# Queries and keys of the last two batches as pairs of float16 parts, turned by DMA, in an attention and expert kernel on one core

## The chip, the cores and the metric

The program runs on one core of a Trainium2 chip. Its engines work side by side, each on its own list of instructions in a fixed order: TensorE (PE; its weight loads are listed as PEld), VectorE (DVE), ScalarE (ACT), GpSimd (POOL), and SyncE (SP), which here does nothing but issue DMAs. They wait for each other by semaphores. The metric is device microseconds of one execution; before the change it is 641.41 us (median of 3 runs, 641.22 to 641.45).

## The reference

Causal attention over 4 batches, 12 heads, 448 positions and 64 elements a head, and behind it a product of two gates and two more matrix products, all in float32:

```
scores = where(mask, -1e9, (q @ k.T) / sqrt(64))
attn   = exp(scores - max) / (sum + 1e-9)
x      = (attn @ v), heads side by side        # 1792 x 768
h      = ((x @ w1) * (x @ w2)) @ w3            # w1, w2: 768 x 1024, w3: 1024 x 1024
out    = h @ w_out                             # 1024 x 768
```

Queries and keys are normal numbers, scaled by 0.7453 and 0.7659, so scores are a few units large and the softmax is not flat.

## The kernel before

First w3 and w_out are multiplied into one matrix (`w34`, L689, float32). Then each batch b goes through two dense stages: `gate(b)` multiplies x by w1 and w2 (L813 to L815: three float16 products for each float32 one, since x and w are kept as a high and a low float16 part), and `project(b)` multiplies by the joined matrix (L873 to L875, three float16 products again). Ahead of each gate, `norms(b)` takes a bound of x (L764, 24 matmuls); it needs x of the whole batch, so its place in the trace shows where the attention of batch b is over.

The attention is cut into 24 pairs of heads, 6 to a batch (`pair`). A pair loads q and k (L403, the helper of every DMA that SP issues), turns them on TensorE (L457: 8 float32 transposes against the identity) and copies them out of PSUM (L461 on ACT or L462 on DVE) into `qkt`, with one head on partitions 0 to 63 and the other on 64 to 127. Scores come in 7 blocks: for each head three of 384, 256 and 128 columns (L495), and one for the last 64 rows of both (L493). Each block is one of the four PSUM banks `sc`. VectorE masks the block, scales it and takes its maximum (L499), which frees the bank; ScalarE takes the exponential (L503); the rows are divided by their sum and split in two float16 parts (`soft`, L528 to L535). The parts are turned by DMA (`pt`, `ptt`) and meet the values in L556 and L561.

Where an instruction stands is set by a planner. `Program.add` takes a due time, the engines that could do the work with a cost each, and what is read and written; `Program.order` then plays the program through and hands each engine a list. The due times come from the numbers in `PLAN`. The result is that pairs of batch b + 1 lie scattered among the gate and projection matmuls of batches b - 1 and b. SP's list is as fixed as the others: a DMA whose data isn't ready holds up all DMAs behind it.

Helpers that matter below: `squares` (ACT: sum of squares, L355), `root_scale` (a one-column float32 matmul against ones, L367, and three small DVE instructions, L370 to L375, that give a power of two near the norm and its inverse), `scaled` (L381 ACT, L382 DVE or L384 POOL: the high float16 part) and `remainder` (DVE, L390: the low part). They serve values and weights before the change.

Of the kernel before, what the change touches and what calls it, by code (L numbers as in the profile page):

```python
# [12 lines left out]
F32 = mybir.dt.float32  # L13
# [13 lines left out]
PLAN = dict(nc=11, wstep=2.3205, soft=49.445, w0=118.4, w34=0.5037, ab=1.5277, out=0.179, gap=16.057, lat=37.703, begin=100.181, wlead=94.567, urgent=13.056, flex=96.023, sc=-27.259, vo=62.311, av=-129.283, x=-15.194, qlead=-18.284, rlead=-5.245, v0=30.056, v1=123.832, gram=2, nf=3, h0=3, hv=5, ns=7, wo0=-132.371, wo1=27.123, wom=21.268, w3a=15.279, w3l=17.856, wd=16.165, wh=-60.261, wl=58.537, fin=8.526, ev=-0.539, po=[-24.2, -29.15, -19.26, 10.49, -17.08, -21.38, -42.72, -39.55, -25.07, -1.21, -22.27, 20.91, 0.72, -56.42, -27.16, -10.64, -22.5, -16.12, -21.26, -21.97, -35.13, 2.64, -7.32, 4.13], wo=[-28.62, 5.45, -16.93, 42.18, 23.33, -12.43, 22.11, -20.21], w3=[-35.5, -43.06, -39.69, 7.92, 8.15, -9.78, -9.89, -29.26], tw=[-16.09, -51.07, -16.26, 0.98, -3.04, -29.34, -21.69, -23.59, -23.52, -22.71, -68.85, 16.04, -16.6, -4.06, -30.21, 7.83], slack=0.7, pflex=42.748)
# [169 lines left out]
def t_mm(n, least=0):  # L197
    return max(n / 2.4 + 2, least) / 1000
# [3 lines left out]
def tile_causal_attention_moe(ctx: ExitStack, tc: tile.TileContext, q, k, v, w1, w2, w3, wo, out):  # L202
    nc = tc.nc
# [32 lines left out]
    def ring(shape, dt, name, n):  # L236
        return Ring(name, fixed(shape, dt, name, n))
# [198 lines left out]
    OFF = (0, P, 3 * P)  # L436
    UP = 2.0**14

    def pair(p):
# [6 lines left out]
        for i, src in ((1, k), (0, q)):  # L446
            dma(qk[0:QP, i], src[b, hs].rearrange("h (p r) d -> p r h d", r=4),
                T - PLAN["qlead"], (), [qkk + (i,)], 2 * S * D * 4, rate=181e3)


        qt, qtk = qkt.next()
        for i in (1, 0):
            ps, key = prog.lease("sc", "tr")

            def turn(i=i, ps=ps):
                for r in range(4):
                    nc.tensor.transpose(ps[:, r:S:4], qk[0:QP, i, r].rearrange("p h d -> p (h d)"), ident[0:QP, 0:QP])  # L457

            prog.add(T + 0.1 * (1 - i), (PE, 4 * t_mm(2 * QP), turn), [qkk + (i,)], [key, qtk + (i,)])
            prog.add(T + 0.5, [  # L460
                (ACT, t_act(S, True), lambda i=i, ps=ps: nc.scalar.copy(out=qt[:, i], in_=ps[:, :S])),  # L461
                (DVE, t_dve(S), lambda i=i, ps=ps: nc.vector.tensor_copy(qt[:, i], ps[:, :S])),  # L462
            ], [key], [qtk + (i,)])

        vs, vsk, _, _ = vsc[b]
        v2, v2k = v16.next()
# [15 lines left out]
        def scores(u, due):  # L482
            i, c, w, lo = place(u)
            ps, key = prog.lease("sc")
            (t32, tk) = heads[i]
            o = t32[:, lo : lo + w]
            m = mask_t if i == 2 else mask[:, (2 - c) * P :]

            def products():
                for j in range(2):  # L490
                    rows = slice(j * D, (j + 1) * D)
                    if i == 2:
                        nc.tensor.matmul(ps[rows, :w], qt[rows, 0, 3 * P : S], qt[rows, 1, 0:w], start=True, stop=True)  # L493
                    elif i == j:
                        nc.tensor.matmul(ps[:, :w], qt[rows, 0, c * P : (c + 1) * P], qt[rows, 1, 0:w], start=True, stop=True)  # L495

            prog.add(due, (PE, 0.9 if i == 2 else max(2 * t_mm(w) + 0.1, 0.31), products),
                     [qtk + (1,), qtk + (0,)], [key, tk + (c,)] + ([tk] if p < 2 else []))
            prog.add(due + 0.4, (DVE, t_dve(w) + 0.09, lambda: nc.vector.tensor_tensor_reduce(  # L499
                out=o, in0=ps[:, :w], in1=m, scale=minus, scalar=-NEG,  # L500
                op0=ALU.add, op1=ALU.min, accum_out=mx[:, u : u + 1])),
                [key, "minus", "mask_t" if i == 2 else "mask"], [mk + (u,), tk + (c,)] + ([tk] if p < 2 else []))
# [394 lines left out]
    with w0 as w0p:  # L897
        w34(w0p)
        for half in range(2):
            at = len(prog.ops)  # L900
            take_v(0, half, starts[0] + PLAN["v0"] + 1.5 * half)
            hold(at, PLAN["hv"] + half)
        for p in range(NP):
            at = len(prog.ops)
            pair(p)
            hold(at, PLAN["h0"] + p)
            if p % 3 == 2:
                take_v(1, p // 3, starts[p] + PLAN["v1"])
# [63 lines left out]
```

## Time and profile before

| what | value |
|---|---|
| median of 3 runs | 641.41 us |
| profiled execution | 642.41 us, span of the trace 640.6 us |
| PE busy | 601.3 us, 94% of the span |
| DVE, ACT, POOL busy | 405.5, 318.7, 175.0 us |
| mean granted TensorE clock | 0.974 of 2.4 GHz |

The trace is of one execution. Spans of matmuls overlap, since they are pipelined, so sums over their mean durations exceed the time they take; the chain of waits, which gives each moment to one instruction, has the time that each one adds.

### The profile page before, as it was taken

The page shows a single profiled execution, that of the slowest core. Times are in us where ns is not written, and L with a number is a line of the kernel's source. Part 1 is how long each engine was busy: PE and PEld are TensorE (multiplying, and loading weights), DVE is VectorE, ACT ScalarE, POOL GpSimd, SP SyncE. Part 2 cuts the span into 40 slices and gives each one's busy share as a digit, 9 for nine tenths or more (in the row PEclk, how much of TensorE's full clock was granted, in tenths as well). Part 3 has the DMA queues.
Part 4 walks back from the last instruction along what each step waited for, and adds up shares of the span by engine and source line. Part 5 has one row for each costly group of instructions (what it writes and reads, how often), then busy time and mean ns, then how long its engine had stood idle before and what let it go on. Part 6 is the DMA issues. An engine that isn't in the chain of part 4 may idle for free.

```text
span 640.6 us, 10699 instructions
## 1 busy us (share of the span) xinstructions
PE 601.3 (94%) x3892; PEld 342.3 (53%) x3892; DVE 405.5 (63%) x1048; ACT 318.7 (50%) x739; POOL 175.0 (27%) x129
## 2 busy tenths in 40 slices
PE   3799969987989999999999999999999999999997
PEld 1454545655545555565655556555555556555564
DVE  7966999999989889866543358846528861212200
ACT  7546988587666867446331336635425441111111
POOL 5643754641554524313100023311102210000000
PEclk9899978988889999999999999999999999999999
DMA  8899596464888949759610139797107616000011
GB/s 340 248 235 226 130 235 169 133 186 111 162 153 170 189 103 154 129 102 185 141 30 19 40 76 176 152 172 143 29 2 150 125 23 124 26 1 1 0 50 49
DMA packets 198836, 78.29 MB, mean 122 GB/s; under 512 B 179840, under 2 KB 195712, under 8 KB 198784
## 3 DMA queue, kind: packets, MB, share of 16 engines
q1 hardware_dynamic: 198784, 77.61, 54.3%
q8 instruction: 30, 0.49, 0.3%
q14 instruction: 22, 0.18, 0.1%
HBM read 43.78 MB, written 5.51 MB: 77 GB/s over the span
## 4 chain that ended last, share of the span: by engine, by line
PE 74%; DVE 14%; issue 5%; ACT 4%; DMA 2%; POOL 0%; SPq 0%; DVEq 0%; ACTq 0%; POOLq 0%
PE sc L495 8%; PE mm L813 7%; PE mm L814 7%; PE mm L815 7%; PE mm L873 4%; PE mm L875 4%; PE mm L874 4%; PE mm L689 3%; PE tr L813 3%; PE tr L814 3%; PE tr L815 3%; PE av L561 3%; PE sc L493 3%; PE sc L689 2%; PE sc L457 2%
## 5 line engine op out<-in xcount | busy, mean ns | idle before, releaser
L532 POOL TENSOR_SCALAR ph<-p,rc 128x256 f16<-128x256 f32 (+2 forms) x47 | 52.8, 1128 | 162.2 <-DVE rc L513 66.4
L814 PE MATMUL mm<-xt,w 128*128 128x448 f16 x258 | 91.4, 354 | 1.9 <-DVE xt L573 1.9
L813 PE MATMUL mm<-xt,w 128*128 128x448 f16 x258 | 91.6, 355 | 0.4 <-ACT xt L570 0.2
L815 PE MATMUL mm<-xt,w 128*128 128x448 f16 x258 | 91.6, 355 | 0.0
L503 ACT ACTIVATE p<-p,mx 128x384 f32<-128x384 f32 (+2 forms) x144 | 71.7, 499 | 37.9 <-DVE mx L499 37.7
L499 DVE CUSTOM_DVE_ANT_0 p<-sc,mask,minus 128x384 f32<-128x384 f32 (+2 forms) x144 | 64.0, 480 | 30.6 <-PE sc L495 29.9
L495 PE MATMUL sc<-qkt 64*128 64x384 f32 (+2 forms) x288 | 72.8, 415 | 5.2 <-DVE mx L499 2.7
L689 PE MATMUL mm<-wof,w3t 128*128 128x384 f32 x192 | 73.3, 522 | 3.5 <-POOL wof L598 3.5
L535 DVE SCALAR_TENSOR_TENSOR ph<-p,rc,ph 128x384 f16<-128x384 f32 (+2 forms) x144 | 67.1, 509 | 3.6 <-ACT ph L530 2.3
L495 PEld LDWEIGHTS sc<-qkt 64*128 64x128 f32 x288 | 41.5, 190 | 40.3 <-issue 9.7
L813 PEld LDWEIGHTS <-w 128*128 128x128 f16 x384 | 38.2, 100 | 38.4 <-issue 5.5
L815 PEld LDWEIGHTS <-w 128*128 128x128 f16 x384 | 37.7, 98 | 38.0 <-issue 3.5
L814 PEld LDWEIGHTS <-w 128*128 128x128 f16 x384 | 37.8, 98 | 30.8 <-issue 1.1
L689 PEld LDWEIGHTS mm<-wof,w3t 128*128 128x128 f32 x192 | 36.6, 203 | 25.8 <-issue 4.7
L873 PE MATMUL mm<-w34h,arena 128*128 128x384 f16 x152 | 49.8, 327 | 0.0
L875 PE MATMUL mm<-w34h,arena 128*128 128x384 f16 x152 | 49.5, 326 | 0.0
L874 PE MATMUL mm<-w34l,arena 128*128 128x384 f16 x152 | 49.5, 326 | 0.0
L813 PE MATMUL tr<-xt,w 128*128 128x448 f16 x126 | 44.9, 357 | 0.0
L814 PE MATMUL tr<-xt,w 128*128 128x448 f16 x126 | 44.9, 356 | 0.0
L815 PE MATMUL tr<-xt,w 128*128 128x448 f16 x126 | 44.9, 356 | 0.0
L839 ACT CAST arena<-g 128x448 f16<-128x448 f32 x21 | 11.8, 564 | 57.4 <-DVE g L834 57.3
L834 DVE SCALAR_TENSOR_TENSOR g<-mm,y,at 128x448 f32<-128x448 f32 x17 | 11.6, 684 | 42.0 <-PE mm L815 41.8
(165 smaller groups left out, 1097.6 us busy)
## 6 DMA issues: line engine op xcount, KB each, us to landing
arena<-in_moe_w_dram SPq DMA_DIRECT2D x11, 768.0 KB, 4.7
qkr<-in_k_dram SPq DMA_DIRECT2D x24, 224.0 KB, 4.0
qkr<-in_q_dram SPq DMA_DIRECT2D x24, 224.0 KB, 4.7
vr<-in_v_dram SPq DMA_DIRECT2D x24, 192.0 KB, 4.3
out_dram<-osb SPq DMA_DIRECT2D x24, 192.0 KB, 2.0
arena<-in_moe_w_dram SPq DMA_DIRECT2D x8, 512.0 KB, 4.4
xt<-in_moe_w_dram SPq DMA_DIRECT2D x5, 768.0 KB, 4.7
arena<-in_moe_w_out_dram SPq DMA_DIRECT2D x3, 768.0 KB, 6.7
```

The source lines that it names most:

```text
L495: nc.tensor.matmul(ps[:, :w], qt[rows, 0, c * P : (c + 1) * P], qt[rows, 1, 0:w], start=True, stop=True)
L499: prog.add(due + 0.4, (DVE, t_dve(w) + 0.09, lambda: nc.vector.tensor_tensor_reduce(out=o, in0=ps[:, :w], in1=m, scale=minus, scalar=-NEG, ...
L503: prog.add(due + 0.9, (ACT, t_act(w, pointers=1, acc=True), lambda: nc.scalar.activation(out=o, in_=o, func=AF.Exp, scale=-1.0, bias=mx[:, ...
L532: (POOL, t_pool(w) + 0.35e-3 * w + 0.16, lambda src=src, r=r, h=h: nc.gpsimd.tensor_scalar(out=h, in0=src, scalar1=r, scalar2=None, op0=AL ...
L535: prog.add(due + 0.4, (DVE, t_dve(w) + 0.06, lambda src=src, r=r, h=h, l=l: nc.vector.scalar_tensor_tensor(out=l, in0=src, scalar=r, in1=h ...
L689: prog.add(due, (PE, 4 * t_mm(NH), lambda: nc.tensor.matmul(ps[:, :NH], w3t[slot(m)][:, g], wof[:, g, ns], start=g == 0, stop=g == KF - 1) ...
L813: nc.tensor.matmul(ps[:, :S], w[:, 0, d], xh, start=d == 0, stop=False)
L814: nc.tensor.matmul(ps[:, :S], w[:, 0, d], xl, start=False, stop=False)
L815: nc.tensor.matmul(ps[:, :S], w[:, 1, d], xh, start=False, stop=d == KD - 1)
L873: nc.tensor.matmul(t, gh[:, fc, cs], w34h[:, fc, ns], start=fc == 0, stop=False)
L874: nc.tensor.matmul(t, gh[:, fc, cs], w34l[:, fc, ns], start=False, stop=False)
L875: nc.tensor.matmul(t, gl[:, fc, cs], w34h[:, fc, ns], start=False, stop=fc == KF - 1)
```

## The change

For batches 2 and 3 (`PLAN["fq"] = 2`, 12 of the 24 pairs) `halved` takes the place of the transposes on TensorE. Queries and keys are loaded with positions on the partitions (three DMAs each where there was one). ACT takes the sum of squares, `root_scale` a scale for the 128 x 512 tile, `scaled` and `remainder` the two float16 parts, and a DMA turns both at once into `qkt`, which is now 512 columns wide. A score block is then three float16 products (high by high, high by low, low by high) that are summed in its PSUM bank; where both heads' blocks are due together, their products alternate. One more small DVE instruction for a pair gives the scale that L499 takes in place of the constant. Batches 0 and 1 keep the old way. One weight chunk fewer is kept in the first memory pool (`nc` 11 to 10), and the planner's numbers are other ones throughout.

```
-PLAN = dict(nc=11, wstep=2.3205, soft=49.445, w0=118.4,
...
+PLAN = dict(nc=10, wstep=1.7166, soft=35.104, w0=98.515,
...
-    qkt = ring([P, 2, S], F32, "qkt", 2)
+    qkt = ring([P, 2, 4 * P], F32, "qkt", 2)
...
+    def halved(p, b, hs, T, qk, qkk, qt, qtk):
+
+        q16 = qt.rearrange("p i f -> p (i f)").bitcast(F16).rearrange("p (i t f) -> p i t f", i=2, t=2)
+        inverse_of = []
+        for i, src in ((1, k), (0, q)):
+            raw_k = [qkk + (i, n) for n in range(3)]
+            for h in range(2):
+                dma(qk[:, i, 0:3, h], src[b, hs.start + h, 0 : 3 * P].rearrange("(c p) d -> p c d", p=P), T - PLAN["qlead"],
+                    [], [raw_k[h]], 3 * P * D * 4, rate=181e3)
+            dma(qk[0:D, i, 3], src[b, hs, 3 * P : S].rearrange("h p d -> p h d"), T - PLAN["qlead"],
+                [], [raw_k[2]], 2 * D * D * 4, rate=181e3)
+            flat = qk[:, i].rearrange("p c h d -> p (c h d)")
+            nat, nk = da.next()
+            n16 = nat.bitcast(F16)[:, : 8 * P].rearrange("p (t f) -> p t f", t=2)
+            am, ak = small(1, "qam")
+            squares(am, flat, lambda n16=n16: n16[:, 1].bitcast(BF16), 4 * P, T - PLAN["hlead"], raw_k, [ak, nk])
+            sc_, sck, e, ek = root_scale([am], [ak], "q", T - PLAN["hlead"])
+            inverse_of.append((e, ek))
+            scaled(n16[:, 0], flat, sc_, 4 * P, T - PLAN["hlead"] + 0.5, raw_k + [sck], [nk])
+            remainder(n16[:, 1], flat, sc_, n16[:, 0], 4 * P, T - PLAN["hlead"] + 1, raw_k + [sck, nk], [nk])
+            dma(q16[:, i].rearrange("p t (c f) -> p (t c) f", f=P), n16.rearrange("p t f -> p (t f)"), T - PLAN["hlead"] + 1.5,
+                [nk], [qtk + (i,)], P * P * 2 * 8, turn=True)
+        iv, ivk = small(1, "qiv")
+        (ek_, kk), (eq_, kq) = inverse_of
+        prog.add(T, (DVE, 0.1, lambda: nc.vector.tensor_scalar(
+            out=iv, in0=ek_, scalar1=eq_, scalar2=-SCALE, op0=ALU.mult, op1=ALU.mult)), [kk, kq], [ivk])
+        return iv, ivk
...
+        halves = b >= PLAN["fq"]
         qt, qtk = qkt.next()
...
+        load = halved if halves else turned_whole
+        iv, ivk = load(p, b, hs, T, qk, qkk, qt, qtk)
...
+            n = min(P, S - c * P)
+
+            def products(qs, ks, start, stop):
                 for j in range(2):
                     rows = slice(j * D, (j + 1) * D)
...
+                    if i in (2, j):
+                        nc.tensor.matmul(ps[rows if i == 2 else slice(0, P), :w], qs[rows, c * P : c * P + n], ks[rows, 0:w],
+                                         start=start, stop=stop)
+
+            if halves:
+                q16 = qt.rearrange("p i f -> p (i f)").bitcast(F16).rearrange("p (i t f) -> p i t f", i=2, t=2)
+                for m_, (a, b_) in enumerate(((0, 0), (0, 1), (1, 0))):
+                    prog.add(due + 0.01 * m_, (PE, t_mm(w) / (1 if i == 2 else 2) + 0.02, lambda a=a, b_=b_, m_=m_: products(
+                        q16[:, 0, a], q16[:, 1, b_], m_ == 0, m_ == 2)),
+                        [qtk + (1,), qtk + (0,)], [key, tk + (c,)] + ([tk] if p < 2 else []))
+            else:
+                prog.add(due, (PE, 0.9 if i == 2 else max(2 * t_mm(w) + 0.1, 0.31), lambda: products(
+                    qt[:, 0], qt[:, 1], True, True)),
+                    [qtk + (1,), qtk + (0,)], [key, tk + (c,)] + ([tk] if p < 2 else []))
...
-                out=o, in0=ps[:, :w], in1=m, scale=minus, scalar=-NEG,
+                out=o, in0=ps[:, :w], in1=m, scale=iv, scalar=-NEG,
...
-            scores(u, T + PLAN["sc"] + 0.3 * n)
+            scores(u, T + PLAN["sc"] + 0.3 * (2 * (n // 2) if halves else n) + 0.001 * n)
```

`turned_whole` holds the old loads and transposes unchanged, and `clear_pads` clears the unused part of the raw tiles once on GpSimd.

TensorE's list before, where a pair of batch 2 is turned during gate 1 (`w_7` is a weight chunk of the gate, `mm` and `tr` its PSUM banks, `sc` the score banks, `qkr` the raw queries and keys):

```order
L815 MATMUL mm_64<-xt_103,w_7_118 128x448
L457 MATMUL sc_69<-ident,qkr_85 128x112 x4
L457 MATMUL sc_68<-ident,qkr_85 128x112 x4
L813 LDWEIGHTS w_7_118
L813 MATMUL mm_64<-xt_103,w_7_118 128x448
```

And now, at one of the two places that a pair has instead (L862 to L864 are the gate lines, `qam` the sum of squares):

```order
L864 LDWEIGHTS w_3_114
L864 MATMUL mm_65<-xt_103,w_3_114 128x448
L367 MATMUL sc_66<-qam_171,ones_77 128x1
L862 LDWEIGHTS w_3_114
L862 MATMUL mm_65<-xt_103,w_3_114 128x448
```

Eight transposes of a pair went from TensorE; two one-column matmuls for each pair came.

TensorE's list before, where the same pair's scores follow:

```order
L815 MATMUL mm_64<-xt_103,w_7_118 128x448
L495 MATMUL sc_66<-qkt_87 128x384
L495 MATMUL sc_67<-qkt_87 128x384
L495 MATMUL sc_69<-qkt_87 128x256
L495 MATMUL sc_68<-qkt_87 128x256
L495 MATMUL sc_66<-qkt_87 128x128
L813 LDWEIGHTS w_8_119
```

And now, at a pair of batch 2 in the same gate:

```order
L864 MATMUL mm_65<-xt_103,w_3_114 128x448
L535 LDWEIGHTS qkt_87
L535 MATMUL sc_67<-qkt_87 128x384
L535 LDWEIGHTS qkt_87
L535 MATMUL sc_68<-qkt_87 128x384
L535 LDWEIGHTS qkt_87
L535 MATMUL sc_67<-qkt_87 128x384
```

Each block of one float32 matmul (two records in the trace, its weight load within) is now three float16 matmuls, those of the two heads by turns, into two banks.

SP's list before, between the projection of batch 0 and the pairs of batch 2 (`pt` and `ptt` are the turned softmax parts):

```order
L403 DMA qkr_84<-in_k_dram 112x8x64
L403 DMA qkr_84<-in_q_dram 112x8x64
L403 DMA_TRANSPOSE pt_97<-ph_95 128x14x128
L403 DMA_TRANSPOSE ptt_100<-pht_96 128x8x128
L403 DMA_TRANSPOSE pt_98<-ph_94 128x14x128
```

And now, where the first pairs of batch 2 are prepared:

```order
L403 DMA qkr_85<-in_q_dram 128x3x64 x2
L403 DMA qkr_85<-in_q_dram 64x2x64
L403 DMA_TRANSPOSE pt_99<-ph_94 128x14x128
L403 DMA_TRANSPOSE pt_97<-ph_95 128x14x128
L403 DMA_TRANSPOSE ptt_100<-pht_96 128x8x128
L403 DMA_TRANSPOSE qkt_86<-da_110 128x8x128
L403 DMA_TRANSPOSE qkt_86<-da_108 128x8x128
```

A pair has six loads and two more transposes on SP where it had two loads; in all SP's transposes go from 72 to 96.

## Rows read from the trace of the kernel before

**Rows 1.** The page's busy time and PE, DVE and clock by slice.

```profile
PE 601.3 (94%) x3892; PEld 342.3 (53%) x3892; DVE 405.5 (63%) x1048; ACT 318.7 (50%) x739; POOL 175.0 (27%) x129
PE   3799969987989999999999999999999999999997
DVE  7966999999989889866543358846528861212200
PEclk9899978988889999999999999999999999999999
```

**Rows 2.** Busy time in stretches cut at the four norms (PE, PEld, DVE, ACT, POOL).

```profile
0.00:208.00 208.00, 176.44 (x867) 103.17 (x867) 181.73 (x394) 145.90 (x309) 105.55 (x75) 0.93 0.76 192
208.00:318.00 110.00, 108.24 (x816) 61.74 (x815) 85.53 (x254) 66.06 (x163) 34.27 (x24) 1.00 0.76 145
318.00:444.00 126.00, 125.15 (x917) 70.76 (x915) 69.07 (x209) 53.53 (x143) 23.67 (x20) 1.00 0.50 99
444.00:550.00 106.00, 105.16 (x815) 59.42 (x812) 56.35 (x165) 39.78 (x102) 11.48 (x10) 1.00 0.39 77
550.00:640.00 90.00, 86.36 (x491) 47.24 (x488) 12.83 (x28) 13.41 (x24) 0.00 (x0) 0.99 0.07 20
```

**Rows 3.** Chain of waits, one pair of batch 2: start us, us, what.

```profile
327.55 0.19 PE tr L815
327.74 0.77 PE sc L457 x8
328.51 0.19 PE tr L813
...
330.22 0.90 PE sc L495 x4
331.11 0.44 DVE p L499
331.55 0.09 issue
331.64 0.10 DVE mx L499
331.73 0.04 issue
331.78 0.48 PE sc L495 x2
332.26 0.29 PE mm L813
332.56 0.19 PE mm L814
332.75 0.19 PE mm L815
332.93 0.42 PE sc L495 x2
333.35 0.90 PE sc L493 x4
```

**Rows 4.** Timeline of that pair's first score blocks on PE.

```profile
330.15 1.35 PE L495 MATMUL sc<-qkt 64*128 64x384 f32 x8
```

**Rows 5.** Chain of waits from 285 to 530 us, shares by line.

```profile
by line: PE sc L495 11.3%; PE mm L813 10.3%; PE mm L814 9.7%; PE mm L815 9.7%; PE mm L873 6.6%; PE mm L875 5.8%; PE mm L874 5.8%; PE tr L813 5.4%; PE tr L814 5.1%; PE tr L815 5.1%; PE av L561 4.8%; PE sc L493 4.6%; PE sc L457 3.4%; PE av L5
```

**Rows 6.** Chain of waits: three float32 matmuls of 384; one block alone.

```profile
28.20 1.94 PE sc L689 x6
380.81 0.84 PE sc L495 x2
```

**Rows 7.** Chain of waits: float16 matmuls with values and in the norms.

```profile
279.93 0.98 PE av L561 x18
317.76 1.31 PE sc L764 x24
```

**Rows 8.** Timeline of PE around a one-column float32 matmul in gate 0.

```profile
223.85 0.35 PE L815 MATMUL mm<-xt,w 128*128 128x448 f16 x1
224.04 0.28 PE L367 MATMUL sc<-wam,ones 128*128 128x1 f32 x2
224.18 0.35 PE L813 MATMUL mm<-xt,w 128*128 128x448 f16 x1
```

**Rows 9.** Groups of instructions: durations on DVE, ACT, POOL and of a weight load.

```profile
L390 DVE SCALAR_TENSOR_TENSOR v<-vr,v_s,v 128x512 f16<-128x512 f32 x24 | 18.2, 760 | 0.6 <-POOL v L384 0.5
L384 POOL TENSOR_SCALAR v<-vr,v_s 128x512 f16<-128x512 f32 x10 | 16.0, 1605 | 32.8 <-PE av L561 27.0 <-DVE rc L513 3.8 <-issue 1.9
L370 DVE TENSOR_SCALAR inv<-sc 128x1 int32<-128x1 int32 x21 | 3.1, 150 | 1.9 <-PE sc L367 1.9
L355 ACT ACTIVATE w<-da 128x768 bf16<-128x768 f32 x16 | 13.3, 834 | 2.8 <-POOL da L598 2.8
L815 PEld LDWEIGHTS <-w 128*128 128x128 f16 x384 | 37.7, 98 | 38.0 <-issue 3.5
```

**Rows 10.** Who PE waited for from 208 us to the end; then SP's queue.

```profile
PE sc L495 <- DVE mx L499: 2.3, 8, 0.3
PE av L556 <- DVE v L390: 0.9, 1, 0.9
PE sc L367 <- ACT w L355: 0.3, 1, 0.3
SPq L403 <- DVE ph L535: 46.2, 20, 15.5
```

**Rows 11.** Timeline of SP in projection 1: start, us in the queue.

```profile
394.99 1.79 SPq L403 DMA_TRANSPOSE ptt<-pht  x1
397.53 0.62 SPq L403 DMA_DIRECT2D qkr<-in_k_dram  x1
```

More of the change, by code (lines that the diff above doesn't have):

```diff
@@ L26 @@
 PE, ACT, DVE, POOL, SP = "PE", "ACT", "DVE", "POOL", "SP"
[L27 removed]
+PLAN = dict(nc=10, wstep=1.7166, soft=35.104, w0=98.515, w34=0.4939, ab=1.864, out=0.1056, gap=7.934, lat=54.674, begin=124.998, wlead=108.279, urgent=16.283, flex=130.436, sc=-28.657, vo=40.18, av=-169.824, x=-3.797, qlead=-32.59, rlead=35.586, v0=19.144, v1=119.702, gram=2, nf=3, h0=3, hv=5, ns=7, wo0=-202.976, wo1=85.211, wom=33.979, w3a=4.552, w3l=33.088, wd=8.804, wh=-51.436, wl=37.619, fin=-41.134, ev=24.84, po=[-24.82, -29.77, -25.56, 9.87, -19.33, -0.94, -43.34, -41.67, -23.49, 5.24, -22.89, 3.16, 5.14, -57.04, -27.78, -11.26, -24.23, -9.57, -25.8, -22.59, -36.97, -12.49, -9.7, 9.83], wo=[-14.34, 44.19, 8.45, 71.74, 57.42, 19.24, 47.18, 16.79], w3=[-59.5, -58.87, -85.5, 5.22, 4.06, -19.4, -19.39, -66.35], tw=[-46.97, -85.5, -45.39, -9.91, -31.02, -57.6, -51.35, -51.53, -46.68, -51.96, -96.47, -10.29, -68.89, -30.15, -61.14, 9.88], slack=0.7, pflex=74.578, fq=2, hlead=23.223)
 HOP = {
@@ L437, in tile_causal_attention_moe, with turned_whole, turn @@
     UP = 2.0**14
+    def turned_whole(p, b, hs, T, qk, qkk, qt, qtk):
+        for i, src in ((1, k), (0, q)):
+            dma(qk[0:QP, i], src[b, hs].rearrange("h (p r) d -> p r h d", r=4),
+                T - PLAN["qlead"], (), [qkk + (i,)], 2 * S * D * 4, rate=181e3)
+        for i in (1, 0):
+            ps, key = prog.lease("sc", "tr")
+            def turn(i=i, ps=ps):
+                for r in range(4):
+                    nc.tensor.transpose(ps[:, r:S:4], qk[0:QP, i, r].rearrange("p h d -> p (h d)"), ident[0:QP, 0:QP])
+            prog.add(T + 0.1 * (1 - i), (PE, 4 * t_mm(2 * QP), turn), [qkk + (i,)], [key, qtk + (i,)])
+            prog.add(T + 0.5, [
+                (ACT, t_act(S, True), lambda i=i, ps=ps: nc.scalar.copy(out=qt[:, i, :S], in_=ps[:, :S])),
+                (DVE, t_dve(S), lambda i=i, ps=ps: nc.vector.tensor_copy(qt[:, i, :S], ps[:, :S])),
+            ], [key], [qtk + (i,)])
+        return minus, "minus"
@@ new lines, in halved @@
+    def halved(p, b, hs, T, qk, qkk, qt, qtk):
+        q16 = qt.rearrange("p i f -> p (i f)").bitcast(F16).rearrange("p (i t f) -> p i t f", i=2, t=2)
+        inverse_of = []
+        for i, src in ((1, k), (0, q)):
+            raw_k = [qkk + (i, n) for n in range(3)]
[20 more added lines that the diff above has]
+        return iv, ivk
@@ L439, in pair, with clear_pads @@
+    def clear_pads(due):
+        for n, t in enumerate(qk_raw.tiles):
+            kk = ("qkr", n)
+            prog.add(due, (POOL, 0.4, lambda t=t: nc.gpsimd.memset(t[D:P, :, 3], 0.0)), [], [kk + (i, *n) for i in range(2) for n in ((), (0,), (1,), (2,))])
     def pair(p):
@@ L445, in pair @@
         hs = slice(2 * hp, 2 * hp + 2)
-        for i, src in ((1, k), (0, q)):
-            dma(qk[0:QP, i], src[b, hs].rearrange("h (p r) d -> p r h d", r=4),
-                T - PLAN["qlead"], (), [qkk + (i,)], 2 * S * D * 4, rate=181e3)
+        halves = b >= PLAN["fq"]
         qt, qtk = qkt.next()
[L452 to L463, printed above, removed]
+        load = halved if halves else turned_whole
+        iv, ivk = load(p, b, hs, T, qk, qkk, qt, qtk)
         vs, vsk, _, _ = vsc[b]
@@ L499, in scores @@
             prog.add(due + 0.4, (DVE, t_dve(w) + 0.09, lambda: nc.vector.tensor_tensor_reduce(
-                out=o, in0=ps[:, :w], in1=m, scale=minus, scalar=-NEG,
+                out=o, in0=ps[:, :w], in1=m, scale=iv, scalar=-NEG,
                 op0=ALU.add, op1=ALU.min, accum_out=mx[:, u : u + 1])),
-                [key, "minus", "mask_t" if i == 2 else "mask"], [mk + (u,), tk + (c,)] + ([tk] if p < 2 else []))
+                [key, ivk, "mask_t" if i == 2 else "mask"], [mk + (u,), tk + (c,)] + ([tk] if p < 2 else []))
@@ L923, in tile_causal_attention_moe @@
             if 1 <= b < B - 1:
+                if b + 1 == PLAN["fq"]:
+                    clear_pads(phase[b] - 20)
                 for p in range((b + 1) * NP, (b + 2) * NP):
```

7 lines of the change are left out of this document (removed).

## The prediction, made before the changed kernel ran

> **What bounds the kernel now.** I read the busy shares first, then busy time by stretch, then the chain of waits, then single groups. The page shows PE busy nine tenths or more in every slice from the thirteenth to the last but one, while DVE falls away [rows 1]. I cut the span at the four norms, since each waits for the attention of one batch [rows 2]. Up to 208 us PE works 176.4 of 208 us and DVE 181.7: PE waits there, mostly for DVE's decoding and splitting. From 208 us on PE works 425 of 432 us at the full clock, and the norms follow as soon as the list reaches them. So the second part lasts as long as PE's work, and a microsecond off that work is a microsecond off the time, as long as nothing new is waited for. All 12 changed pairs lie between about 285 and 530 us, in that part. PE's waits there are small: 2.3 us for score banks, 0.9 for a DVE part, 0.3 for one sum of squares [rows 10].
>
> **What leaves PE.** One pair shows the pattern [rows 3]. Eight transposes take 0.77 us. Four blocks follow, then PE waits 0.67 us (331.11 to 331.78) until DVE has freed a bank, then 0.48 and 0.42 us for the two blocks of 128 and 0.90 for the tail. The first gate matmul behind a score group has 0.29 us where the others have 0.19: 0.10 for leaving. For all 12 pairs I take the shares of the chain from 285 to 530 us [rows 5]: of 245 us, L495 has 11.3%, L493 4.6%, L457 3.4%, together 47.3 us. Six of the pairs show the wait for a bank, 0.67 each, 4.0 us. The order has 33 separate score groups for them, so leaving costs 3.3. Sum of what the old way takes: 54.6 us.
>
> **What comes to PE.** Rates first. Float32 costs 4 cycles a column: three matmuls of 384 in 1.94 us are 0.647 each, and 4 x 384 / 2.4 GHz is 0.640 [rows 6]. A block alone took 0.84, so entering a score group costs 0.20. Do the two heads, on different halves of the rows, run at once? Blocks of 384, 384, 256 and 256 would take 2.13 us one after the other and 1.07 side by side; they took 1.35 with entering and the pipeline's drain [rows 4]. So they overlap nearly fully, in float32. Float16 costs one cycle a column: 18 matmuls of 4608 columns in all, on two halves of the array's columns, took 0.98 us [rows 7], half of their 1.92.
>
> The order has, for the 12 pairs, 66 matmuls of 384 columns by turns with the other head, 60 of 256 and 12 of 128, and in one-headed groups 6 of 384, 15 of 256 and 57 of 128; and 72 tail matmuls of 448, which alternate. With full overlap of those that alternate that is 21.1 us, with none 36.6. I take 21.1, since float32 on row halves and float16 on column halves both show it. There are 38 separate groups: entering 7.6, leaving 3.8 us. The wait for banks I leave at 4.0: VectorE frees a bank no faster than before, and the order puts 3 or 6 gate matmuls (0.57 us or more) before the blocks that need one. The 24 one-column matmuls cost 0.14 each, if their sum is there: from 224.04 to 224.18 [rows 8]; 3.4 us. Sum 39.9 us, 14.7 less than 54.6.
>
> By the Trainium skill (TensorE: Matmul & The Clock Gate, Part 3), four row tiles gave 3.07 of 4 in a measurement there; estimated with that share the 21.1 would be 27.5 and the forecast 6.4 us later. The trace's own ratio for two tiles is better than that.
>
> **What comes to the others.** A pair gains on DVE two remainders at 0.76 and seven small instructions at 0.15 [rows 9], 2.6 us, less a part of its two copies. For six pairs that is 15 us on 69.1 of 126 and on 56.4 of 106 [rows 2]: cover enough. Of the 24 scalings 10 go to GpSimd at 1.6 us; it works 23.7 and 11.5 us in these stretches. The sums of squares on ACT cost 0.8 for 768 columns, less for 512, and replace copies. SP's list gains two transposes of about 1.8 and four loads of at most 0.62 for each pair [rows 11], 36 us a batch. Data of the new pairs has a longer way: load, square, one-column matmul, three small steps, two splits, a transpose. PE's list now holds 24 matmuls that wait for ACT and 12 first blocks that wait for a DMA. Each was put there by a planner, so some will come late: bounds are 0 (only 0.3 us of such a wait on that part now) and, if each of the 24 waited as long as the 0.9 for a DVE part, 22. I take 1.5, near the rows that show almost none. Behind a waiting matmul stand gate matmuls, and nothing can pass it.
>
> **The first part** is rewritten by the planner's numbers and by the weight chunk that moves behind the joined product. Counted in the order, PE's matmuls ahead of the first norm are the same in number and kind (15 of each gate line in both), DVE has 402 entries for 404. So its work is equal, only the waits can differ: at best DVE's 26 idle microseconds vanish, at worst another gap like PE's largest opens, 5 us a piece. I take 0, with 6 either way as the usual error.
>
> Sum: the profiled execution, 642.4 (a span of 640.6 and 1.8 around it), less 14.7 plus 1.5 is 629.2. That execution was 1.0 slower than the median, so 628.2 beside a median of 641.4.
>
> **Rivals.**
> 1. The first part comes out better, by the new order: its waits shrink by 6 to 13 us, 615 to 622. For it: 31.6 us of PE's time there are idle. Against: nothing in the change takes work from DVE there.
> 2. It comes out worse by 6 to 12: 634 to 640.
> 3. Float16 blocks of one head don't hide their weight loads. The order has 78 matmuls in one-headed groups; at 0.098 a load [rows 9] that is 7.6 us more, 636. Against: the norms' 24 matmuls, all on the same rows, took 1.31 us, of which their 2688 columns are 1.12; unhidden loads would have added 2.4 [rows 7]. The Trainium skill (the same page and part) says that a weight load overlaps a running matmul only if its row group differs. The norms' row disagrees, so the chance is small.
> 4. The heads don't overlap in float16: 36.6 for 21.1, 15.5 more, 643.7. The change then saves nothing on PE.
> 5. Slower: SP's queue becomes the bound in the second and third stretch. A batch has 18 transposes now, 12 loads and some 16 values and outputs: at 1.79 and 0.62 [rows 11] 50 of 126 us in the second; with 36 more, 86 of a stretch shortened to 119. Each of the 12 new transposes of a batch holds the list until its remainder is there. A wait for `soft`'s remainders is 46.2 / 20 = 2.3 us [rows 10]; the list is full at (119 - 86) / 12 = 2.75. From there it decides: at 3.6 us a wait it is 129, 10 more than the stretch, in both stretches 20, so 628 + 20 = 648. Against: before, such waits were mostly time in which nothing else was due.
>
> **How the numbers follow.** Forecast (622 to 634) 0.56; rival 1 0.12; rival 2 0.10; rival 3 0.05; rival 4 0.04; rival 5 0.13. Range 617 to 641: it leaves out most of rivals 4 and 5 and the far end of 1. A measurement here can't tell less than 0.2%, 1.3 us, from no change. Faster: 0.56 + 0.12 + 0.08 + 0.05 = 0.81. The same: 0.05, the ends of rivals 2, 4 and 5 about 641. Slower: 0.14.
>
> **What would show it.** Right: from the first norm to the end PE stays busy in all but 2% of the time, and that part is 12 to 15 us shorter; the groups of a pair (384, 384, 256, 256) take about 1.0 to 1.1 us with entering; a one-column matmul in the gate moves the stream by 0.14. Wrong: triples by turns at 0.32 us each for 384 columns (rival 4), one-headed triples of 128 near 0.45 us (rival 3), PE idle before L367 or before the first block of a pair, with SP's list behind it (rival 5), or a first norm that isn't at 208 us (rivals 1 and 2).

## The result, and the profile after

The changed kernel takes 617.23 us (median of 4 runs, 616.59 to 617.67) beside 641.32 us for the kernel before in the same comparison. The ratio is 0.9637, with a 95% interval of 0.9612 to 0.9663: 24 us less, where 13 were forecast. The profiled execution took 616.59 us with a span of 614.8.

The page first: busy time, then PE, DVE and the clock by slice, to be held against [rows 1].

```profile
PE 579.4 (94%) x3940; PEld 328.6 (53%) x3940; DVE 422.5 (69%) x1135; ACT 335.6 (55%) x795; POOL 206.9 (34%) x144
PE   2899879999699999999999999999999999999997
DVE  6976988999889979888158877963698970222100
PEclk9999988999689999999999999999999999999999
```

PE is busy 21.9 us less, in more instructions, and DVE 17 us more. The second view is busy time in stretches cut at the four norms (length, then PE, PEld, DVE, ACT, POOL, clock, share of DMA, GB/s), as in [rows 2]:

```profile
0.00:204.00 204.00, 174.11 (x872) 101.53 (x873) 179.83 (x394) 144.63 (x308) 114.14 (x77) 0.94 0.79 194
204.00:306.00 102.00, 100.97 (x790) 58.10 (x788) 79.45 (x235) 63.64 (x156) 35.99 (x26) 1.00 0.86 161
306.00:419.30 113.30, 113.30 (x928) 63.02 (x927) 81.14 (x258) 62.14 (x167) 28.62 (x21) 1.00 0.69 131
419.30:523.30 104.00, 103.78 (x855) 57.90 (x853) 69.27 (x221) 51.19 (x139) 28.19 (x20) 1.00 0.61 115
523.30:614.00 90.70, 87.26 (x506) 48.07 (x504) 12.83 (x28) 13.99 (x25) 0.00 (x0) 0.99 0.06 20
```

The stretches were 208, 110, 126, 106 and 91 us, and are 204, 102, 113, 104 and 91. (One pair's scores moved from the stretch up to the second norm into the one behind the third, which is why the fourth stretch shrinks little.) From 306 us on PE is busy nearly all the time while pairs run, although DVE has 12 us more in the third stretch (81.1 for 69.1, six pairs' scores in both) and 13 more in the fourth (five pairs' scores where it was four).

One pair in the chain of waits (start us, us, what), to be held against [rows 3]:

```profile
318.33 0.19 PE mm L864
318.52 0.92 PE sc L535 x12
319.44 0.31 PE tr L367 x2
319.75 0.21 PE mm L862
...
320.34 0.35 PE sc L535 x6
320.69 0.29 PE mm L862
...
321.36 0.69 PE sc L535 x6
322.05 0.30 PE mm L862
```

The eight transposes are gone. The four large blocks are one unbroken group of 12 matmuls in 0.92 us, and no instruction of DVE stands in the chain between the score groups, where 0.67 us of DVE stood before (PE itself was idle for 0.28 of them, as the part on the prediction shows). The first gate matmul behind a group still has 0.29 to 0.30.

In the timeline of the same pair a root of the next pair stands between two gate matmuls as in [rows 8]: the stream that had 0.19 us a matmul shifts by 0.14 (322.56 to 322.70).

```profile
322.37 0.35 PE L864 MATMUL mm<-xt,w 128*128 128x448 f16 x1
322.56 0.28 PE L367 MATMUL sc<-qam,ones 128*128 128x1 f32 x2
322.70 0.35 PE L862 MATMUL mm<-xt,w 128*128 128x448 f16 x1
```

And who PE waited for from 200 us to the end (us in total, times, longest), as in [rows 10]. The first of these waits falls ahead of the first norm:

```profile
PE av L605 <- DMA ptt<-pht: 1.1, 1, 1.1
PE sc L367 <- ACT da L355: 1.0, 1, 1.0
PE sc L535 <- DVE mx L548: 0.2, 1, 0.2
```

The waits for banks fell from 2.3 to 0.2, and of the 24 new roots one came late, by 1.0.

### The profile page after: what moved, and what is told of

The parts are those of the page before. It is cut to its first block, busy times and chain, and to the rows that moved or that the text cites. A ratio compares the mean times of both kernels' runs of the same rounds, so it can differ in the third digit from the quotient of the medians.

```text
span 614.8 us, 11067 instructions
## 1 busy us (share of the span) xinstructions
PE 579.4 (94%) x3940; PEld 328.6 (53%) x3940; DVE 422.5 (69%) x1135; ACT 335.6 (55%) x795; POOL 206.9 (34%) x144
## 4 chain that ended last, share of the span: by engine, by line
PE 63%; DMA 3%; DVE 2%; ACT 2%; issue 1%; POOL 1%; SPq 0%; ACTq 0%; POOLq 0%; DVEq 0%
PE mm L862 8%; PE mm L863 7%; PE mm L864 7%; PE sc L535 6%; PE mm L922 4%; PE mm L924 4%; PE mm L923 4%; PE tr L862 3%; PE tr L863 3%; PE tr L864 3%; PE av L610 3%; PE tr L922 2%; PE tr L924 2%; PE tr L923 2%; DMA pt<-ph 2%; PE av L605 2%
## 5 line engine op out<-in xcount | busy, mean ns | idle before, releaser
L862 PE MATMUL mm<-xt,w 128*128 128x448 f16 x270 | 95.9, 355 | 0.0
L863 PE MATMUL mm<-xt,w 128*128 128x448 f16 x270 | 95.4, 353 | 0.3 <-DVE xt L622 0.3
L864 PE MATMUL mm<-xt,w 128*128 128x448 f16 x270 | 95.5, 354 | 0.0
L535 PE MATMUL sc<-qkt 64*128 64x128 f16 (+6 forms) x480 | 80.5, 366 | 1.6 <-DVE mx L548 1.6
L738 PE MATMUL mm<-wof,w3t 128*128 128x384 f32 x192 | 74.9, 521 | 2.7 <-POOL wof L647 2.6
L584 DVE SCALAR_TENSOR_TENSOR ph<-p,rc,ph 128x384 f16<-128x384 f32 (+2 forms) x144 | 76.4, 577 | 1.4 <-POOL ph L581 0.7
L581 POOL TENSOR_SCALAR ph<-p,rc 128x256 f16<-128x256 f32 (+2 forms) x41 | 46.7, 1144 | 58.2 <-DVE rc L562 17.1
L862 PEld LDWEIGHTS <-w 128*128 128x128 f16 x384 | 39.4, 102 | 36.0 <-issue 5.0
L864 PEld LDWEIGHTS <-w 128*128 128x128 f16 x384 | 37.5, 98 | 35.9 <-issue 1.0
L384 POOL TENSOR_SCALAR v<-vr,v_s 128x512 f16<-128x512 f32 x19 | 33.6, 1768 | 52.8 <-PE av L610 39.7
L384 POOL TENSOR_SCALAR da<-qkr,q_s 128x512 f16<-128x512 f32 x10 | 15.9, 1592 | 105.2 <-DVE qiv L483 97.5
L862 PE MATMUL tr<-xt,w 128*128 128x448 f16 x114 | 40.3, 354 | 0.0
L864 PE MATMUL tr<-xt,w 128*128 128x448 f16 x114 | 40.2, 353 | 0.0
L863 PE MATMUL tr<-xt,w 128*128 128x448 f16 x114 | 40.2, 353 | 0.0
L548 DVE CUSTOM_DVE_ANT_0 p<-sc,mask,qiv 128x384 f32<-128x384 f32 (+2 forms) x72 | 31.0, 480 | 10.7 <-PE sc L535 10.5
L548 DVE CUSTOM_DVE_ANT_0 p<-sc,mask,minus 128x384 f32<-128x384 f32 (+2 forms) x72 | 32.7, 476 | 7.3 <-PE sc L535 7.3
```

Of the source, the lines that this page charges most:

```text
L384: (POOL, t_pool(n) + 0.35e-3 * n + 0.16, lambda: nc.gpsimd.tensor_scalar(out=dst, in0=src, scalar1=s, scalar2=None, op0=ALU.mult)),
L535: nc.tensor.matmul(ps[rows if i == 2 else slice(0, P), :w], qs[rows, c * P : c * P + n], ks[rows, 0:w], start=start, stop=stop)
L584: prog.add(due + 0.4, (DVE, t_dve(w) + 0.06, lambda src=src, r=r, h=h, l=l: nc.vector.scalar_tensor_tensor(out=l, in0=src, scalar=r, in1=h ...
L738: prog.add(due, (PE, 4 * t_mm(NH), lambda: nc.tensor.matmul(ps[:, :NH], w3t[slot(m)][:, g], wof[:, g, ns], start=g == 0, stop=g == KF - 1) ...
L862: nc.tensor.matmul(ps[:, :S], w[:, 0, d], xh, start=d == 0, stop=False)
L863: nc.tensor.matmul(ps[:, :S], w[:, 0, d], xl, start=False, stop=False)
```

## The experiments

Twelve kernels ran. This table has, for each, the median time, the start of the four norms on PE in its profile, the span, and the time from the first norm to the end of the span. Each profile is of one execution. The first part differs among them (202.2 to 208.6 us among kernels with the changed planner numbers, ten chunks and no halves in batch 1), so the last column tells more than the span. The planner plays every edited program through anew, so the order of the instructions differs a little from kernel to kernel as well.

| kernel | us | norms at | span | behind first norm |
|---|---|---|---|---|
| before | 641.32 | 208.3, 317.6, 443.2, 549.1 | 640.6 | 432.4 |
| after | 617.23 | 203.8, 306.0, 419.3, 523.2 | 614.8 | 411.0 |
| e1 none halved | 637.31 | 205.5, 314.4, 439.1, 545.2 | 636.7 | 431.2 |
| e6 one batch halved | 628.89 | 202.2, 311.2, 435.0, 532.2 | 624.2 | 422.0 |
| e2 old numbers | 634.05 | 206.7, 313.6, 443.4, 548.3 | 631.8 | 425.1 |
| e8 eleven chunks | 625.61 | 215.7, 313.6, 428.6, 537.2 | 623.1 | 407.4 |
| e3 heads apart | 618.96 | 208.6, 310.7, 424.4, 528.4 | 619.9 | 411.3 |
| e5 one product | 606.76 | 204.5, 305.8, 415.7, 521.2 | 604.6 | 400.1 |
| e10 remainder twice | 615.50 | 202.9, 305.0, 430.9, 522.1 | 613.6 | 410.7 |
| e11 turn twice | 630.47 | 205.3, 307.2, 429.9, 545.3 | 628.8 | 423.5 |
| e14 loads twice | 622.52 | 203.7, 305.6, 420.3, 535.9 | 619.4 | 415.7 |
| e13 15 pairs | 620.54 | 204.4, 311.8, 423.6, 532.3 | 618.9 | 414.5 |
| e7 18 pairs | 649.80 | 209.8, 338.1, 464.0, 557.2 | 649.0 | 439.2 |
| e12 18 pairs, early | 648.00 | 206.4, 344.7, 459.0, 564.1 | 647.9 | 441.5 |

**How much is the halves, how much the numbers.** e1 keeps the new planner numbers and halves nothing.

```
-PLAN = dict(nc=10, wstep=1.7166, ..., fq=2, hlead=23.223)
+PLAN = dict(nc=10, wstep=1.7166, ..., fq=4, hlead=23.223)
```

> The changed kernel with no pair halved (fq = 4): all 24 pairs turned on TensorE in float32, under the new planner's numbers. Theory A, that PE's work from the first norm on sets the time and that the new numbers only shorten the first part: the first norm stays near 203.7 us as in the changed kernel, and from there to the end it takes 430 to 434 us as before, so 636 to 640 us. Rival, that most of the gain is the new numbers' order: 617 to 625 us.

637.31 us, ratio 0.9951 [0.9933, 0.9970]: the numbers alone give some 3 us. By the spans most of it lies ahead of the first norm (2.8 us; behind it 1.2). Its third and fourth stretch, in the columns of the stretches above, are those of the kernel before:

```profile
314.40:439.10 124.70, 123.86 (x907) 69.71 (x905) 69.30 (x216) 52.88 (x140) 24.32 (x19) 1.00 0.55 104
439.10:545.20 106.10, 105.25 (x812) 59.64 (x810) 57.62 (x162) 38.11 (x100) 10.58 (x10) 1.00 0.37 72
```

e6 halves only the last batch (`fq=3`).

> Only the last batch has float16 halves; the planner's numbers are those of the changed kernel. Theory A (the gain behind the first norm is PE's own time, a fixed amount for each of the twelve pairs, about 1.8 us): half of 21 us is kept, so about 627 us (625 to 630), and the stretch from the second to the third norm is about 125 us again with the one behind it near 104 and the stretch from the first to the second near 103 or 109 by where the pairs stand. Rival (the gain comes from the order that the planner's numbers make, and the halves only fit into it): the time moves little from 617 or goes to 634 and over.

628.89 us, ratio 0.9817 [0.9777, 0.9857]. Behind the first norm it takes 422.0 us, 9.2 less than e1, which has the same numbers, and the second batch of halves takes another 11.0. That is 1.5 to 1.8 us for each of the twelve pairs. PE's busy time in that part goes the same way, 424.4 in e1, 415.8 here and 405.5 in the changed kernel: a saving of PE's own work by the pair, as theory A had it. The fourth stretch came out at 97 us and not 104, since the saving falls where the pairs stand.

e2 goes the other way: the halves with the numbers of before (eleven chunks among them).

```
-PLAN = dict(nc=10, wstep=1.7166, soft=35.104, ...
+PLAN = dict(nc=11, wstep=2.3205, soft=49.445, ..., fq=2, hlead=23.223)
```

> The changed kernel with the planner's numbers of before (nc = 11 included) and fq = 2, hlead = 23.223: the mechanism alone. Theory A: the first norm at 208 us as before, and the part behind it shorter by about 20 us, 617 to 624 us. Rival, that the gain is the new order's: 632 us or more. If the old numbers start the longer chain of a halved pair too late, PE waits before first blocks and the time is between the two, and the trace shows the waits.

634.05 us, ratio 0.9897 [0.9866, 0.9928]: slower than theory A expected, and of the 21 us behind the first norm only 7 are there. The first fence is PE's timeline ahead of the third norm (idle us and its releaser in brackets), the second the busy time of the stretch around it, in the columns of the stretches above:

```profile
429.90 0.38 PE L367 MATMUL sc<-qam,ones 128*128 128x1 f32 x2 [2.32 <-ACT da L355]
431.65 0.35 PE L863 MATMUL mm<-xt,w 128*128 128x448 f16 x1 [1.16 <-DVE xt L622]
438.76 0.57 PE L605 MATMUL av<-ptt,v 128*64 128x64 f16 x24 [2.29 <-DMA ptt<-pht]
442.92 0.58 PE L367 MATMUL sc<-qam,ones 128*128 128x1 f32 x2 [2.25 <-ACT da L355]
```

```profile
432.00:448.00 16.00, 10.74 (x109) 7.20 (x109) 11.41 (x41) 8.59 (x24) 2.13 (x2) 0.79 0.84 160
```

Two roots, an attention product and a gate matmul come late, 8 us in all; the mean granted clock of the 16 us around the norm is 0.79 of full speed, between its two levels of 1.2 and 2.4 GHz, so work done then takes longer too. Behind the first norm PE is idle for 15.5 us here and for 5.5 in the changed kernel; that is 10.0 of the 14.1 us between them, and the rest is busy time. So the numbers (the chunk count with them) are worth 3 us by themselves, and 14 behind the first norm as cover for the halves. Which of the numbers give that cover was not tried.

e8 keeps everything but the count of weight chunks ahead of the joined product (`nc=11`).

> The changed kernel with eleven weight chunks ahead of the joined product, as before the change, in place of ten. Theory A (the chunk only moves work of VectorE about within the first part, as the prediction took it): the first norm is 203 to 209 us and the time 614 to 622. Rival (the chunk that moves behind the joined product is what made the first part shorter): the first norm comes at 208 us or later by 3 to 5 us in every profile and the time is 620 to 624.

625.61 us, ratio 0.9779 [0.9731, 0.9827]. The first norm comes at 215.7, later than in any other run. The timeline names the wait: the sum of squares of a weight, twice.

```profile
159.99 0.59 PE L367 MATMUL sc<-wam,ones 128*128 128x1 f32 x2 [4.58 <-ACT w L355]
204.26 0.59 PE L367 MATMUL sc<-wam,ones 128*128 128x1 f32 x2 [5.81 <-ACT w L355]
```

These two are 10.4 of the 11.9 us by which the first norm is later; behind it the kernel takes 3.6 us less, with 13 of PE's matmuls moved ahead of that norm in the list. So the chunk is not the free move of work that I took it for: with these numbers its old place costs 8 us. With the old numbers eleven chunks gave 208.3 and 206.7, so the count and the numbers belong together. Why exactly this weight comes late was not traced further.

**What a score group costs.** e3 gives the three products of a block one after the other, in place of by turns with the other head.

```
-            scores(u, T + PLAN["sc"] + 0.3 * (2 * (n // 2) if halves else n) + 0.001 * n)
+            scores(u, T + PLAN["sc"] + 0.3 * n + 0.001 * n)
```

> The changed kernel with the blocks of a pair due one after the other, so that a block's three products stand together and the heads no longer alternate (384: three of one head, three of the other). If a matmul on the other rows may start as soon as the one ahead of it has started (overlap in order), only the last product of a block overlaps the first of the next: the group of 384, 384, 256, 256 takes 1.17 + 0.12 us where it took 0.92, 0.37 more, and 11 such pairs give 4 us: 620 to 623 us. With no overlap at all between heads the group takes 1.6 + 0.12, 0.8 more: 625 to 628 us. If order doesn't matter (the hardware looks ahead): 616 to 618 us and groups of 0.92.

618.96 us, ratio 0.9671 [0.9632, 0.9711], and 411.3 us behind the first norm for 411.0. The chain gives the four large blocks the time they had:

```profile
338.60 0.93 PE sc L535 x12
```

Three matmuls of one head, then three of the other, take as long as six by turns, and not the 1.29 us of an overlap in the order of the list. So the order of the two heads does not matter inside a group.

e5 leaves out the two cross products (queries high by keys low, and the reverse), so that a block is one matmul.

```
-                for m_, (a, b_) in enumerate(((0, 0), (0, 1), (1, 0))):
+                for m_, (a, b_) in enumerate(((0, 0),)):
```

> The changed kernel with one product a block instead of three: only high by high, the two cross products are left out, so scores lose their low parts. Theory A (PE's work sets the time): two thirds of the 21.1 us of columns go, 14 us, so 602 to 605 us. Rival (after the change VectorE or SP's queue sets the pace in the stages with pairs): 611 us or more.

606.76 us, ratio 0.9478 [0.9441, 0.9514]: 10.9 us less behind the first norm, a little short of theory A's 12 to 15. The same four blocks, now four matmuls, in the chain:

```profile
320.60 0.38 PE sc L535 x4
```

Against 0.92 for twelve, 8 matmuls of 384 and 256 columns (2560 in all) cost 0.54 us. At one column a cycle they would be 1.07 one after the other and 0.53 side by side, so the two heads overlap wholly in float16. What is left of either group beyond its columns, 0.12 of 0.92 and 0.11 of 0.38, is the cost of entering. All twelve pairs' products have 21.1 us of columns, two thirds of them 14.1. The order of e5 has 47 separate groups for 38 (9 by about 0.22 for entering and leaving is 2.0), and from the first norm on PE is idle 6.9 us for 5.5: together 3.4, which covers the difference to 10.9.

**What the others can bear.** e10 computes each remainder of queries and keys twice on VectorE.

```
             remainder(n16[:, 1], flat, sc_, n16[:, 0], 4 * P, T - PLAN["hlead"] + 1, raw_k + [sck, nk], [nk])
+            remainder(n16[:, 1], flat, sc_, n16[:, 0], 4 * P, T - PLAN["hlead"] + 1, raw_k + [sck, nk], [nk])
```

> Each remainder of a changed pair is computed twice on VectorE: 24 more instructions of about 0.76 us, 18 us, and the halved queries and keys are there 0.8 us later each. Theory A (VectorE's added work is hidden beside PE, as the prediction took it): 616 to 620 us. Rival (VectorE or the longer chain sets the time): 4 to 18 us more, 621 to 635, with PE idle before the first block or the root of a pair.

615.50 us, ratio 0.9612 [0.9558, 0.9666], 410.7 us behind the first norm: no cost. The remainders of queries and keys take 36.4 us of VectorE for 18.1. VectorE's added work is covered, with room for as much again.

e11 issues each DMA transpose of queries and keys twice.

> Each DMA transpose of halved queries and keys is issued twice, one after the other: 24 more on SyncE's list, at about 1.8 us each 22 us in a batch's stretch. By the prediction's count the list then has about 108 of 113 us in the second stretch. Theory A (there is still room): under 620 us. Rival (the queue becomes the bound as the prediction's fifth rival had it): 625 to 650 us, with PE waiting for turned values or queries and SyncE's list behind it.

630.47 us, ratio 0.9828 [0.9789, 0.9866], 12.5 us more behind the first norm. The first fence is SP's list ahead of the third norm (start, us in the queue), the second PE's timeline there:

```profile
407.73 4.63 SPq L403 DMA_TRANSPOSE pt<-ph  x2
412.59 3.02 SPq L403 DMA_TRANSPOSE qkt<-da  x2
415.70 1.29 SPq L403 DMA_TRANSPOSE ptt<-pht  x1
417.09 2.68 SPq L403 DMA_TRANSPOSE qkt<-da  x2
419.83 2.29 SPq L942 DMA_DIRECT2D out_dram<-osb  x2
```

```profile
419.18 0.57 PE L607 MATMUL av<-ptt,v 128*64 128x64 f16 x24 [0.58 <-DMA ptt<-pht]
423.16 0.99 PE L537 MATMUL sc<-qkt 64*128 64x384 f16 x12 [2.42 <-DMA qkt<-da]
```

The list has hardly a gap from 407.7 to 422 us, and PE waits for what it brings. That looked like the fifth rival: a full queue. e14 fills the list by as much with other transfers: the six loads of a changed pair are issued twice.

```
+                for _ in range(2):
                     dma(qk[:, i, 0:3, h], src[b, hs.start + h, 0 : 3 * P].rearrange("(c p) d -> p c d", p=P), T - PLAN["qlead"],
```

> Each of the six loads of queries and keys of a changed pair is issued twice: 72 more plain loads at 0.6 us on SyncE's list, 22 us a batch, as much of the list as the 24 doubled transposes of the run that took 630 us, and 5.4 MB more. Theory A (SyncE's list is what the doubled transposes filled): 626 to 635 us. Rival (what cost there was the transposes' own way, their place late in the chain of a pair behind which the list holds; loads due long before are free): 616 to 621 us.

622.52 us, ratio 0.9719 [0.9694, 0.9743]: between the two theories, nearer the rival. In the timeline between the second and the third norm SP's issues add up to 57 of 125.5 us before, 78 of 113.3 after, 97 of 122.7 in e11 and 99 of 114.6 in e14. The fullest list of the four, e14's, kept PE at work all the way:

```profile
305.60:420.20 114.60, 114.60 (x925) 63.17 (x923) 83.94 (x271) 58.93 (x159) 30.12 (x25) 1.00 0.77 151
```

So the sum on the list does not decide. Behind the first norm PE's idle time is 16.0 us in e11 and 6.8 in e14, for 5.5 in the changed kernel. In the changed kernel's trace the last load of a pair is issued 16 to 56 us ahead of the pair's first block, its last transpose 5 to 7 us ahead. A doubled load is not needed soon; a transpose stands late in the chain of a pair, and PE is the next to need it, which is how I read the difference (the two runs differ in the kind of transfer as well). What e14 lost (4.7 us) is 3.4 of busy time of PE, in an order with 45 separate score groups for 38, and 1.3 of idle time; its one long wait, 1.7 us, is for a turned softmax part.

**More of the same.** If each pair saves 1.8 us, the pairs of batch 1 should too. e7 halves batches 1 to 3 (`fq=1`, and the pads cleared earlier).

> Batches 1 to 3 have float16 halves, not only 2 and 3. Theory A (PE's own time): the six pairs of batch 1 save about 1.8 us each on PE, 10.5 us, where PE is the bound. Those pairs run from about 160 to 320 us, of which the part up to the first norm is bound by VectorE; about four of the six lie behind it. So at most 606 to 612 us. Rival (VectorE and the longer chain decide there): batch 1's halves add about 15 us to VectorE, which has 87 of 110 us busy in the stretch from 196 to 306 and is fuller before it; what falls before the first norm moves that norm by as much as it adds, up to 7 us later, and PE waits for late halves: 617 to 630.

649.80 us, ratio 1.0119 [1.0086, 1.0151]: 1.2% slower than the kernel before. First the timeline of PE ahead of the second norm, then busy time there, in the columns of the stretches:

```profile
316.84 4.13 PE L535 MATMUL sc<-qkt 64*128 64x384 f16 x24 [3.61 <-DMA qkt<-da]
325.67 0.38 PE L367 MATMUL sc<-qam,ones 128*128 128x1 f32 x2 [2.07 <-ACT da L355]
335.35 0.85 PE L605 MATMUL av<-ptt,v 128*64 128x64 f16 x24 [2.62 <-DMA ptt<-pht]
```

```profile
314.00:340.00 26.00, 16.56 (x154) 9.78 (x155) 20.55 (x72) 15.90 (x46) 7.31 (x5) 0.67 0.83 157
```

PE waits for turned queries, for a square, for turned probabilities, and its granted clock is 0.67 in these 26 us. The six pairs' steps come late one behind the other. e12 tries the plain cure, a lead of 40 us for every halving (`hlead=40.0`).

> Batches 1 to 3 halved as in the run that took 649.8 us, with every halving due 40 us ahead of its pair in place of 23.2. Theory A (that run lost its time because halves, turned weights and probabilities came late, and a longer lead mends it): PE's waits behind the first norm shrink from about 18 us to under 5, and the time falls to 608 to 620 us. Rival (the lists of VectorE and SyncE are too full in that stretch whatever the lead): 635 us or more; earlier halving then only pushes other work of VectorE later.

648.00 us, ratio 1.0121 [1.0104, 1.0137]: the lead does not mend it. PE's waits behind the first norm are still 18.5 us, the longest (4.8 us) again for turned queries. That the lists of VectorE and SyncE are too full, as the rival has it, is not shown by this. e13 halves three pairs more, those from the middle of batch 1 on.

```
-        halves = b >= PLAN["fq"]
+        halves = p >= 9
```

> Float16 halves from the fourth pair of batch 1 on (15 pairs in place of 12); those three pairs stand behind the first norm. Theory A (1.8 us less of PE for each pair, where PE sets the time): 617 less 5.3 is 612 us (610 to 614). Rival (the longer chains of these pairs come late with an order that is not fitted to them, as in the run with three batches): 618 to 630, with PE waits for halves, turned probabilities or values between the first norm and the second.

620.54 us, ratio 0.9675 [0.9653, 0.9698]: the rival again. From the first to the second norm, PE is idle for 5.2 of 106.7 us, for after's 1.0 of 102:

```profile
205.00:311.70 106.70, 101.45 (x819) 56.90 (x817) 91.10 (x270) 64.19 (x158) 37.27 (x23) 1.00 0.79 150
```

Among the versions with all three products none beats the changed kernel (615.50 for e10 can't be told from it). Whether due times fitted to 15 or 18 pairs would was not tried.

## Why the prediction was right, and where its sizes were off

The direction, the place and the mechanism held: the gain is PE's own time in the twelve pairs, behind the first norm (e1, e6). The time lies 0.2 us inside the low end of the range, outside the forecast's own 622 to 634, so that it lies in the range at all is partly luck. By spans, the first part gave 4.5 us where 0 was taken, the rest 21.3 where 13.2 were. Busy time behind the first norm, before and after, parts the 21.3 into work and waiting:

```profile
208.20:640.60 432.40, 424.71 (x3027) 239.16 (x3025) 223.64 (x653) 172.59 (x431) 69.42 (x54) 1.00 0.45 89
203.80:614.80 411.00, 405.51 (x3075) 227.30 (x3073) 242.89 (x744) 190.97 (x487) 92.81 (x67) 1.00 0.57 110
```

PE's work fell by 19.2 us where 14.7 were forecast, and its idle time by 2.2, from 7.7 to 5.5, where a rise of 1.5 was.

- **Columns, 21.1 us with full overlap: right.** e5 measured 2560 columns in 0.54 us. Rival 4 falls with it. By the 3.07 of 4 in the Trainium skill (TensorE: Matmul & The Clock Gate, Part 3) they would have taken 0.69, as an estimate; the two heads here do better, and the measurement decides.
- **Entering, 38 groups by 0.20: mis-sized, 2.5 us.** The 0.20 came from a float32 block. In the chain from 280 to 530 us L535 has 10.0% of 250 us, 25.0 (first line below). For a stretch the chain runs over other engines (second line) while PE does a group of 12 (third line, from the timeline) and a triple of 128. With 0.92 and 0.27 for these L535 has 26.2, less 21.1 of columns: 5.1 for entering, 0.13 each, where 7.6 were forecast.

```profile
by line: PE mm L862 11.4%; PE mm L863 10.4%; PE mm L864 10.4%; PE sc L535 10.0%; PE mm L922 7.7%; PE mm L924 7.1%; PE mm L923 7.1%; PE av L610 5.1%; PE tr L862 4.6%; PE tr L863 4.3%; PE tr L864 4.3%; PE tr L922 3.2%; PE tr L924 3.1%; PE tr 
477.49 1.57 POOL v L384
479.73 0.99 PE L535 MATMUL sc<-qkt 64*128 64x384 f16 x12
```

One likely reason, argued and not tested: what can't be hidden at a group's start is its first weight load, and the trace of after has 0.19 us for float32 (L367) and 0.095 for float16.
- **Bank waits, kept at 4.0: wrong, 3.8 us.** Two steps failed. The 0.67 us of a pair was read off the chain as PE's wait. But the chain follows DVE from the end of the first two blocks on, while PE still does the other two: the four keep it busy for 1.35 us from 330.15 [rows 4], and the timeline before has 0.28 of idle time ahead of the fifth:

```profile
331.78 0.48 PE L495 MATMUL sc<-qkt 64*128 64x128 f32 x2 [0.28 <-DVE mx L499]
```

Six of these are 1.7 us; the other 2.3 of the 4.0 were work on the old blocks, which left with them, and the sum of what comes to PE has them once more. And that the wait would stay because "VectorE frees a bank no faster" was beside the point: 0.2 us is left of it. In e1 the 1.7 us are still there, in 6 places, so it is the halves and their order that take them away, not the numbers alone: in most pairs gate matmuls now follow the four large blocks.
- **Leaving 0.10 and the roots 0.14: right** by the rows of one pair above, for a root between gate matmuls. Nine of the 24 roots stand right behind a score group and take 0.31 in the chain, in which most of that group's leaving is contained.
- **The allowance of 1.5 for the longer chain: 1.0 was needed** for the one late root. But e2 shows that this is the planner's work: with the old numbers the chain costs 14 us. I read it from a row of the kernel before and from the order; the order alone could not have told.
- **What the terms come to.** Of work, 2.5 for entering and 2.3 for the old blocks are 4.8, for the 4.5 between 19.2 and 14.7. Of waiting, the score banks fell by 2.1 (2.3 to 0.2), the 0.9 and 0.3 of [rows 10] are gone, and the late root costs 1.0: 2.3 less, for the 2.2 measured. The terms were read on one execution each, so a part of so close a sum is luck. Behind the first norm e1 takes 1.2 us less than before without any halves, so not all of it is theirs.
- **The first part, 0 with 6 either way: inside.** e1's comparison puts it at about 3 us, with the numbers and not the halves as the cause. (PE's largest gap there was 8.1 us, on GpSimd, and not the 5 that the prediction names.) Rival 1's price came true and its reason did not: the first part gave 3 to 4.5 us and not 6 to 13.
- **VectorE, covered: right; 15 us a batch was too much.** Behind the first norm it has 19.3 us more for both batches (242.9 for 223.6), and e10 added 18.3 of remainders for nothing. GpSimd took 10 of the 24 scalings, at 1.59 us each.
- **Rival 3, loads of one head not hidden: falls.** A one-headed triple of 128 took 0.27 us in the chain, not 0.45.
- **Rival 5, SP's queue: the estimate of the list was near (78 of 113 us; forecast 86 of 119) by two errors that partly cancel, 50 for the 57 us before and 36 for the 21 that came; the mechanism was not.** e11's 630 us looked like it, but e14 with a fuller list took 622. The runs point to which DMA is late, not to how full the list is.

## What to carry to other kernels

Size the cost of switching from a row of the same type: entering a score group cost 0.20 us in float32 and 0.13 in float16. Time that the chain of waits gives to another engine is not idle time of the bound engine: hold it against the idle time in the timeline before it is put into a sum. When a change lengthens the chain of data behind a bound engine, ask whether the order leaves it time: the same operations gave 7 us or 21 behind the first norm by the planner's numbers alone, and extending them to 18 pairs without new numbers lost all of it. Ask of a queue which of its entries the bound engine needs next, and only then how full it is.

## What was not expected of the hardware

Two heads on different halves of the array's rows overlap as well in the order A A A B B B as by turns: 0.93 and 0.92 us for twelve matmuls (e3). And waits can cost more than their own length: in e2 PE waited 8 us in four places ahead of the third norm, and the norm's 24 matmuls behind them took 2.40 us in the chain, for 1.31 before [rows 7]. The granted clock in the norm was 0.50, the lower of the two levels:

```profile
442.92 0.58 PE sc L367 x2
443.50 2.40 PE sc L813 x24
443.40:446.00 2.60, 2.60 (x26) 2.30 (x27) 1.64 (x6) 0.72 (x1) 0.00 (x0) 0.50 0.62 137
```

The first line is the last late root, the second the norm, the third busy time there with the clock, in the columns of the stretches. In e11 PE waited 2.42 us for turned queries, and the clock behind that wait (423.1 to 425 us) was 1.00, so not every wait does this.
